# Two pairs of heads of batch 0: fp16 weight pairs turned by DMA in place of fp32 weights turned on TensorE, in a tuned attention + Mish MLP kernel

## The chip, the core and the metric

The kernel runs on one core of one Trainium2 chip. The metric is the device time of one execution in microseconds (us), the median over several runs. The core has five instruction streams: TensorE for matrix products (PE in the views, PEld for its weight loads), VectorE (DVE), ScalarE (ACT), GpSimd (POOL) and SyncE (SP), which here only issues DMA transfers. Each stream runs its instructions in the order in which the program holds them, and an instruction that waits holds up all that stand behind it on its stream.

## What is computed

Rotary attention over 4 batches, 8 heads, 576 positions of 64 numbers, and then an MLP with a Mish-like gate on the 2304 rows of 512 numbers that come out of it. All inputs and the output are fp32.

```python
q_rot, k_rot = (rotate(q), rotate(k))
scores = scale * np.matmul(q_rot, k_rot.transpose(0, 1, 3, 2))
scores = scores - np.max(scores, axis=-1, keepdims=True)
attn = np.exp(scores)
attn = attn / (np.sum(attn, axis=-1, keepdims=True) + 1e-09)
attn_out = np.matmul(attn, v)                # (4, 8, 576, 64)
x = attn_out.transpose(0, 2, 1, 3).reshape(2304, 512)
h = x @ w_in                                 # 512 x 2048
g = h * np.tanh(np.where(h > 20.0, h, np.log1p(np.exp(np.minimum(h, 20.0)))))
return g @ w_out                             # 2048 x 512
```

## The kernel before

**Attention.** The heads are taken in pairs, `P` = 0 to 15; pairs 0 to 3 are batch 0. One `step(P, t)` handles 128 queries of a pair; the fifth step, t = 4, handles the last 64 queries of two pairs at once. A step multiplies on PE (`scores`, line 502, into the two PSUM buffers `pair`), takes row maxima on DVE (L510), exponentials with their sums on ACT (L512, into `e`), and the inverse of the sums on DVE (L520, L522). The weights must then be turned, so that the keys lie on partitions, before `av` can multiply them by V. There are two ways:

- Batch 0 (`exact` in the code): `turned` turns the fp32 `e` by PE against a unit matrix (L546, and L561 for the last 64 keys), turns the inverse sums too (L563), and ACT or DVE copy the results out of PSUM into `et` and `ew` (L555/L556, L570/L572, L574/L576). `av` multiplies in fp32 (L630, L632, L633). DVE then multiplies by the inverse sums (L661), and `x` is written as a sum of two fp16 parts: the high part by L664 or L666, the rest on DVE (L669).
- The other batches: `weights_hi` writes weights times inverse sum as fp16 (L527 on POOL, L529 on ACT or L530 on DVE), `weights_lo` writes what fp16 lost as a second fp16 (L534, always DVE), a DMA issued by SP turns both at once (L617, from `ew` into `et`), and `av` makes three fp16 passes (L638, L642, L643), with V as an fp16 pair too (`load_v`, L463 to L467). The high part of `x` then comes straight from PSUM (L664 or L666), the rest by L669.

`av(P, k)` covers the first 256 queries (k = 0) or the last 320 (k = 1). `et` has two buffers and `ew` three, used in turn.

**MLP.** A chunk c is half a batch: 256 or 320 columns. `mlp_h` makes 16 groups of 12 matmuls (L877), the Mish on ACT (L882) and the fp16 pair `g` (L892/L893, L896); `mlp_p` makes 16 groups of 12 matmuls (L913) and writes the output. The weights arrive as fp32 and are taken apart into fp16 pairs by `decode` (L755 to L775), in the first third of the kernel. For batch 0 the two h chunks stand before the two p chunks in the plan's numbering, but PE's order mixes them with attention: h of the first 256 columns, then p of those, then h of the last 320 columns, which needs `x` of all four pairs with k = 1.

**Order.** Every operation has a number. A table, `ORDER`, lists the numbers in the order in which they are issued; a letter chooses one of the engines that an operation allows, `@` the PSUM banks, and `+m` puts m idle matmuls against the unit matrix (L1026) ahead of the operation on PE. All engines' streams follow from this one list.

Of the kernel before, what the change touches and what calls it, by code (L numbers as in the profile page):

```python
# [10 lines left out]
F32 = mybir.dt.float32  # L11
# [12 lines left out]
NP = H // 2  # L24
# [25 lines left out]
AVL = 3  # L50
PREP = [7, 5, 0, 13]
# [13 lines left out]
    205b 103@1 148 186@3 229@0 146 202 36 206 147 188 34 257b 150 233 149 251b 153@4+6 40 207 235 208 151 189 43 236@2
    104 237 37 230 458 105@3 41 238 285 192@2 35 107@1 245b 239 209 154 194 51 240@0 190 152 46 214@54 241 195 108 191
    109 106 242 286 244@0 157@1 203 196 215 159 158 287 216 217 288@2+6 197 155@3 357 289 218 246 169@1 52 170 297b
    290 356 270@54+3 459 250@2 247 156 47 291 172 256@1 273 292@0 337@3 271 274 49 252 272 293 220 253 231 53 248 258
    224@4 254 338 50 222@0 219 259 54 280@2 48 225 378 278@3 303b 309 322@54 460 223 221 275 377 55 529 281 279 226@1
    262@0 325 263 276 323 326 56 277 264 324 282@2+9 462 232 608 341@45 294 284 265 227 283 575 461 266 330@3 249  # L70
    296@2 342 373@0 18 344 228 331 394 379 343 463 315 339 406 298 637 345 349@1 267 464 613 327 374 260 465@3 530 328
    386 380@0 329 347 346 350 334@4 466 255 348 171 467 375 381 353@3 468 336 299 335 314@1 469@0 400 382 295 351@5
    387 383 355 470 354 316 412 384@2 352 332@0 385 317 308@3 358@45 376 333 120 389 310 617 300 454@2 361 302@1 638
    359 390 362 304 360 311 614 368@5 305 393@0 455 366@3 369 395 1 456 418@45 340 306 457 31 396 261 367 526@1 419
    411@2 307 421 420 635@0 210 363 243 422 413 211 527 414 667@4 312b 183 301b 426@3 550 313 636 546@2 268 471 364
    668 472 365 388 423 405@1 609 549 606@5 415 407 547 408 703@0 607 212 665b 399@2 701b 666 409 435@45 427b 410 704
    318 401 370@1 436 610 684@0 372 397 371b 402 416 437 213 438 428@3 825@1 615 429b 766 702 439 806@2 398b 826 424
    618 441 440 511@45 442 425 709 434 685 789@3 514 807 403 269 833b 430@1 804b 790 319b 449@0 515 431b 404 432b
    443@2 512 446@3 805 433 1094@1 450b 611 513 448 531@54 445 834 451 444 453 760 640 452b 447 829@2 532 499 474 533
    521@0 612 827 602@3 534 641 522 705 473 44 710 535 830 537 516 764 475 517 713 581c 476@0 603 541@5 518 487b 639  # L80
    477 539@3 391 320 478 542 479 523@2 714 540 480@0 57 880@4 711 481 604 536 525b 321 706 765 484 538 505 524b 519@3
    493b 828 543@0 881 482 520 605 831@5 483 545b 707b 504@2 544b 708 498@3 661@0 506 832 762 507 500 508 719 486@4
    501 839 509 502 488 914@2 878 662 503 489 492@3 587@54 915 879 528 616 494 490 835@0 590 918 491 495 591 1109 919
    588 842 837@2 485 723 589 840 392 510 593 836 620@45 548 1110 621 838 592 551 622 916b 595@3 917 597@0 623 552@2
    1137 553 624 554 555 496b 596 556@2 497 642@45 557 594 417 626 558 1138b 559 598 569 599@3 645 716 574@2 563 628@1
    718 643 601 0 1139 1140@0 576 600 577 1154 769 629b 568@3 578b 562@2 560 1155 579 646 564 570 663 1182 843 644 565
    625 571 630@1 1183 627 664 754b 669@54 647 566b 631 722 567 580@2 650@3 648 672 632@0 651 670 841 652 1185@1 673
    633b 572b 970 649 634 582 573 671 656@3 583 686@45 736 653@0 689 717 1199 654b 690 971 657b 748c 660 584 785@2 687
    659b 688 655b 585 720 712 691 692 561 675 721 972 658b 724 973 725@0 786 677@5 726 787 679@3 727 678 728 974 694@2
    680 729@0 772@45 695 1043 730 674 586 693 731 788 732 619 676 735@3 696@0 775 1200 742b 737 697 738 1184 681@2  # L90
    747@0 739b 1239 773 1044 776 682b 683b 774 749 698@3 1046 1240 791@54 699b 741@2 777 750 1045 1241 778 743 821@1
    700 751 740 794 753@0 744 795 752 792 745 779 755 781b 857 797 756 1242@3 793 768 746b 757 783 808@45 780b 733 758
    822 796 1256 823 798 811 799b 882 782 800b 1257 809 861 812 734 759 1281 810 886 802 824 883 844@54 888 801 784
    884 814 920@2 715 845 885 813 887 846 922@0 815 1282b 817b 1047 847 890 858 889 848 803 943@1 849 923 850 761 819
    864@54 859 944 891 862 921 964@3 1201 851 941 867 816 994 892 998 853 865 939@0 965 852c 868 855 958@1 818 942 820
    866 854 893@2 1048 901@45 870 990 1002 959b 894 869 995 960 924@3 904 999 856 871 895 905 896 902 988@2 1003 903
    1049b 925 897@1 873c 968@5 898 1000 899 872c 940 907 992@1 989 900 906 966b 1283 908 874 969 875 1020 1018@3 909b
    996b 876 967 926@45 911 993 910b 997 1156 1088@0 929 1019 1115 863 927 930 912 1041@2 1111 1321 1039b 1040 928
    961@1 1202b 1004 991 1089 931 1021 945@54 913 932 933 1203b 1042 934c 935b 1070@3 1204 946 962 963 947 948 1037@0
    1157 1334 877 949 936 1066@2 1038 937 951 1118 975@54 938 1335 860 1071 1022@1 1116 976 1067 950 1090 952 978 1159  # L100
    1284@0 1023 953b 1092b 977 1301 1068b 1093 1091 1085@3 979 955 954b 1069 1005@54 980 956 981 957 982 1302 1216 983
    1008 1006 984 1009 985 1317 1007 986 1338 1217 1119 1024@45 1011 987 1086b 1318 1010 1012 1117 1320@2 1027 1014
    1025 1028 1013 1339 1362 1026 1160 1030 1112 1029 1016 1001 1050@54 1015 1120 1319 1031 767 1033 1032b 1063@1 1053
    1158 1051 1054 771 1121 1052 1034 1113 1017 1072@45 1056 1322 1055 1035 1161 1363 1114 1075 1073 1076 1057 1036
# [178 lines left out]
def attention_mish_mlp(ctx: ExitStack, tc: tile.TileContext, qk, v, vflat, rope, ident_in, w_in, w_out, outT):  # L283
# [807 lines left out]
```

## Time and profile before

| | |
|---|---|
| time before, median of 3 runs | 614.68 us (614.17 to 615.95) |
| the profiled execution | 615.46 us, of which the span from first to last instruction is 613.7 us |
| PE busy in the span | 592.6 us (97%) |
| DVE / ACT / POOL busy | 447.2 / 390.9 / 239.9 us |
| mean granted TensorE clock | 0.997 of full speed |

A busy share counts an instruction from its start to its end. PE's instructions overlap in the array, so its share says little of how closely they follow each other; for that the starts of neighbouring rows are compared.

### The profile page before, as it was taken

Reading aid. Unit: us, or ns where it says so; the run is one execution under the profiler, and the core shown is the slowest. Engines: PE = TensorE matmul, PEld = TensorE weight load, DVE = VectorE, ACT = ScalarE, POOL = GpSimd, SP = SyncE. Lnnn points to the kernel's source line nnn. Section 1 sums busy time; section 2 is a strip of 40 time slices with the busy share of each in tenths; the row PEclk is TensorE's granted clock in tenths of the full one; section 3 lists DMA queues with packets and bytes.
Section 4 is the critical chain, followed back from the end, with each engine's and each line's share of the span. In section 5 each row is a group of like instructions: output and inputs, shape, how many; then the busy total and the mean of one; then the engine's idle time right before and its main releaser. Section 6 shows DMA issues by size and latency. Waiting matters only on the chain. (4 is left out here: it accounts for less than half of the span.)

```text
span 613.7 us, 12945 instructions
## 1 busy us (share of the span) xinstructions
PE 592.6 (97%) x5112; PEld 442.8 (72%) x5112; DVE 447.2 (73%) x964; ACT 390.9 (64%) x771; POOL 239.9 (39%) x218
## 2 busy tenths in 40 slices
PE   5889999999999999999999999999999999999997
PEld 4655776776666666788877767887877778887775
DVE  4999998998899989678788976678878754320320
ACT  3799998978879665587768454765689534311400
POOL 2989567556645555341762006208221010000000
PEclk9989999999999999999999999999999999999999
DMA  9977234242879689917792866355745773100000
GB/s 341 409 296 263 76 112 160 69 151 70 209 178 237 133 184 204 194 21 155 181 168 40 193 122 135 90 117 101 129 89 87 139 136 69 31 10 1 27 12 33
DMA packets 143436, 82.49 MB, mean 134 GB/s; under 512 B 128144, under 2 KB 133904, under 8 KB 141712
## 3 DMA queue, kind: packets, MB, share of 16 engines
q1 hardware_dynamic: 138768, 76.95, 52.1%
q10 hardware_dynamic: 4608, 4.72, 2.3%
q8 instruction: 40, 0.66, 0.4%
q14 instruction: 20, 0.16, 0.1%
HBM read 45.09 MB, written 4.72 MB: 81 GB/s over the span
## 5 line engine op out<-in xcount | busy, mean ns | idle before, releaser
L913 PEld LDWEIGHTS <-w 128*128 128x128 f16 x1536 | 147.2, 98 | 46.2 <-issue 9.8
L877 PEld LDWEIGHTS <-w 128*128 128x128 f16 x1536 | 148.0, 98 | 42.8 <-issue 7.2
L913 PE MATMUL bank<-g,w 128*128 128x320 f16 (+1 forms) x1344 | 176.0, 288 | 0.0
L877 PE MATMUL bank<-xt,w 128*128 128x320 f16 (+1 forms) x1284 | 166.8, 286 | 0.1
L512 ACT ACTIVATE e<-pair,mx 128x576 f32<-128x576 f32 x144 | 105.8, 738 | 66.8 <-DVE mx L510 61.4
L510 DVE TENSOR_REDUCE mx<-pair 128x1 f32<-128x576 f32 x144 | 104.9, 747 | 27.9 <-PE pair L502 27.6
L386 POOL TENSOR_TENSOR raw<-raw,cs 128x576 f32<-128x576 f32 (+2 forms) x62 | 94.3, 1538 | 74.3 <-DMA raw<-in_qk 70.3
L534 DVE SCALAR_TENSOR_TENSOR ew<-e,rs,ew 128x576 f16<-128x576 f32 x108 | 104.8, 988 | 4.5 <-ACT ew L529 3.4
L502 PE MATMUL pair<-qk 64*128 64x288 f32 (+1 forms) x704 | 84.2, 366 | 1.1 <-ACT e L512 0.5
L527 POOL TENSOR_SCALAR ew<-e,rs 128x576 f16<-128x576 f32 x33 | 27.0, 819 | 146.2 <-DVE rs L522 79.8
L882 ACT ACTIVATE mh<-bank,cells 128x320 f32<-128x320 f32 (+1 forms) x107 | 50.5, 498 | 37.7 <-PE bank L877 25.1
L502 PEld LDWEIGHTS pair<-qk 64*128 64x128 f32 (+1 forms) x704 | 54.3, 181 | 21.5 <-issue 10.1
L896 DVE SCALAR_TENSOR_TENSOR g<-mh,cells,g 128x640 f16<-128x640 f32 (+1 forms) x56 | 49.2, 894 | 14.6 <-ACT g L892 14.4
L893 DVE TENSOR_SCALAR g<-mh,cells 128x640 f16<-128x640 f32 (+1 forms) x32 | 16.9, 533 | 51.3 <-ACT mh L882 35.5
L529 ACT ACTIVATE ew<-e,rs 128x576 f16<-128x576 f32 x44 | 33.7, 769 | 15.5 <-issue 9.8
L643 PE MATMUL bank<-et,v 128*64 128x256 f16 (+1 forms) x288 | 39.8, 288 | 0.0
L642 PE MATMUL bank<-et,v 128*64 128x256 f16 (+1 forms) x288 | 39.8, 288 | 0.0
L642 PEld LDWEIGHTS <-v 128*64 128x64 f16 x288 | 29.6, 110 | 8.4 <-issue 5.7
L882 ACT ACTIVATE mh<-pair,cells 128x256 f32<-128x256 f32 (+1 forms) x21 | 10.4, 495 | 36.8 <-PE pair L877 31.8
L877 PE MATMUL pair<-xt,w 128*128 128x256 f16 (+1 forms) x252 | 33.9, 284 | 0.0
L882 ACT ACT_TABLE_LOAD x24 | 30.8, 1283 | 1.4 <-DVE xt L896 0.4
L390 POOL TENSOR_TENSOR raw<-raw 128x288 f32<-128x288 f32 x32 | 31.1, 985 | 0.3
(142 smaller groups left out, 770.2 us busy)
## 6 DMA issues: line engine op xcount, KB each, us to landing
raw<-in_qk SPq DMA_DIRECT2D x30, 576.0 KB, 4.5
w<-in_w_out SPq DMA_DIRECT2D x5, 1024.0 KB, 5.2
g<-in_w_in SPq DMA_DIRECT2D x4, 1024.0 KB, 6.5
w<-in_w_in SPq DMA_DIRECT2D x4, 1024.0 KB, 8.8
stg<-in_v SPq DMA_DIRECT2D x8, 320.0 KB, 4.0
out_dram<-ot ACTq DMA_DIRECT2D x16, 160.0 KB, 2.2
stg<-in_vflat SPq DMA_DIRECT2D x6, 384.0 KB, 3.8
qk<-in_w_out SPq DMA_DIRECT2D x4, 512.0 KB, 4.7
```

Source lines behind the costliest of these rows:

```text
L386: e.tensor_tensor(out=t()[:, :, s], in0=t()[:, :, s], in1=cs()[:, :, s], op=ALU.mult)
L502: nc.tensor.matmul(pts[h]()[to, c, :HS], x[own, q], y[own, s], **kw)
L510: op((DVE, dve_ns(S), lambda: nc.vector.tensor_reduce(m(), pt()[:, :, :HS], axis=AX.XY, op=ALU.max, negate=True)), w=[m], r=[pt])
L512: op((ACT, act_ns(S, psum=True, ptr=2) + 35, lambda: nc.scalar.activation(e().rearrange("p (c s) -> p c s", c=2), pt()[:, :, :HS], AF.Exp, ...
L529: (ACT, act_ns(S, ptr=1) + 25, lambda: nc.scalar.activation(w()[:, c], e(), AF.Copy, scale=r()[:, h:h + 1])),
L534: op((DVE, dve_ns(S) + 130, lambda: nc.vector.scalar_tensor_tensor(out=w()[:, c], in0=e(), scalar=r()[:, h:h + 1], in1=w()[:, hc], op0=ALU ...
L642: nc.tensor.matmul(po()[0:64, :n], V()[:, vi, c, 0:64], et[:, c, :], start=False, stop=last)
L643: nc.tensor.matmul(po()[64:128, :n], V()[:, vi, c, 64:128], et[:, 5 + c, :], start=False, stop=last)
L877: nc.tensor.matmul(hp(), w1()[:, wi, cc, f:f + 128], x()[:, xi, cc, q0:q0 + n], start=cc == 0 and a == 0, stop=cc == NCC - 1 and a == 2)
L882: op((ACT, act_ns(n, psum=True, ptr=1) + 60, lambda j=j, hp=hp: nc.scalar.activation(hn()[:, j, :n], hp(), AF.Mish, scale=uh())), w=[(hn, ...
L896: op((DVE, dve_ns(2 * n) + 61, lambda: nc.vector.scalar_tensor_tensor(out=gv()[:, 1, f, :n], in0=hn()[:, :, :n], scalar=f32(gs), in1=gv()[ ...
L913: nc.tensor.matmul(pp()[:, :n], w2e[e]()[:, wi, f], gv()[:, gi, f % 4, :n], start=f == 0 and a == 0, stop=f == NF - 1 and a == 2)
```

## The change

A new constant `NX = 2` says for how many pairs of batch 0 the last 320 queries keep the exact way. Pairs 2 and 3 lose it for k = 1, that is for five steps: t = 2 and 3 of each, and their shared t = 4. V of these two pairs is read from memory a second time and taken apart into an fp16 pair (`cast_v`, at two new places of the program). And `ORDER` is another table throughout: other places, engines, banks and fills.

```diff
+NX = 2
@@ load_v
-        t, flat = v_stage(P // NP)
+        cast_v(P)
+
+    def cast_v(P):
+        t, flat = v_stage(max(1, P // NP))
...
-        st["V", P] = o
+        st["H", P] = o
@@
+    def exact(P, k):
+        return P < NP and (k == 0 or P < NX)
+
@@ places
-            et_tile(p, k, *((F32, 9) if P < NP else (F16, 18)))
-            if P < NP:
+            et_tile(p, k, *((F32, 9) if exact(p, k) else (F16, 18)))
+            if exact(p, k):
@@ step
-        exact = P < NP
+        own = exact(P, int(t > 1))
         to = places(P, t)
-        ew = None if exact else sbuf((128, 4 * S), F16, "ew", EW)
+        ew = None if own else sbuf((128, 4 * S), F16, "ew", EW)
...
-        if exact:
+        if own:
             turned(es, [(st["ET", p, k], at, t, st["R", p, k], q) for p, k, at, q in to], r)
             return
@@ av
-        V = st["V", P]
+        V = st["V" if exact(P, k) else "H", P]
@@
         at(2 * P - 4, load_v, P)
     at(VA, v_amax, 0)
+    for P in range(NX, NP):
+        at(12 + P, cast_v, P)
@@ ORDER, two of its rows
-    59 2 58 3 5 11 6 4 20 140b 111 12 134c 94 122b 110 128b 19 112 113@0+16 32 7b 114 115 116 117@1+7 118 13 119 9
+    588 509 492@3 830@2 502 545b 544b 494 486@1 503 660@0 495 589 484 590 528 912 637 496b 591 488 497 831 592 717
```

In what follows the changed kernel's lines stand 3 to 8 further down than before: scores are L505, the maxima L513, `weights_lo` L537, the turning DMA L623, fp16 `av` L644/L648/L649, the second MLP product L919, the fills L1034.

On PE, in the stretch of the second MLP product of batch 0's first 256 columns, before the change (`e_...` are the exponentials of single heads, `bank` and `pair` PSUM buffers):

```order
L913 MATMUL bank_73<-stg,w_68 128x256
L546 MATMUL bank_74<-ident,e_1444 128x128 x4
L502 MATMUL pair_78<-qk 128x288
L502 MATMUL pair_77<-qk 128x288
...
L546 MATMUL bank_76<-ident,e_1560 128x128 x4
L561 MATMUL bank_73<-ident,e_1415 64x128
L561 MATMUL bank_73<-ident,e_1444 64x128
L563 MATMUL bank_73<-ident,rs 64x128 x2
L913 LDWEIGHTS w_68
```

The same stretch with the change:

```order
L919 MATMUL bank_73<-stg,w_68 128x256
L1034 LDWEIGHTS ident
L1034 MATMUL pair_78<-ident 128x256
...
L505 MATMUL pair_78<-qk 128x288
L505 MATMUL pair_77<-qk 128x288
...
L919 LDWEIGHTS w_68
L919 MATMUL bank_73<-stg,w_68 128x256
```

The turning groups are gone between the MLP groups; ahead of four operations here stand fills, of 5, 5, 5 and 4 matmuls, one of which is shown. The whole program holds 147 fill matmuls where it held 124.

On DVE, the end of the exact work of these two pairs before the change:

```order
L510 TENSOR_REDUCE mx<-pair_78 128x1
L556 COPY et<-bank_73 128x4x64
L572 COPY et<-bank_76 128x64
L759 TENSOR_SCALAR raw<-raw 128x512
L510 TENSOR_REDUCE mx<-pair_77 128x1
L572 COPY et<-bank_76 128x64
L556 COPY et<-bank_73 128x4x64
L722 TENSOR_REDUCE cells<-qk 128x1
```

And with the change, about there:

```order
L537 SCALAR_TENSOR_TENSOR ew<-e_1566,rs,ew 128x576
L537 SCALAR_TENSOR_TENSOR ew<-e_1521,rs,ew 128x576
L513 TENSOR_REDUCE mx<-pair_78 128x1
L513 TENSOR_REDUCE mx<-pair_77 128x1
L767 SCALAR_TENSOR_TENSOR bank_74<-bank_74,qk 128x512
L537 SCALAR_TENSOR_TENSOR ew<-e_1650,rs,ew 128x576
L537 SCALAR_TENSOR_TENSOR ew<-e_1645,rs,ew 128x576
L770 SCALAR_TENSOR_TENSOR qk<-qk,bank_74 128x512
```

Copies out of PSUM have given way to two L537 for each step, ten in all. Counted between the first L877 matmul on 256 columns and the first on 320 in the list, DVE has these differences: nine L534 more (the tenth comes after), four more pieces of `decode` (L761, L764, L775), six L572, five L893, two L661, three L836 and one each of L556, L759 and L922 fewer, and four more of the shortest (L336, L520, L522); L893's five went to ACT as L892.

On SP, the first turning DMAs with the change, among the loads of weights and of q and k:

```order
L715 DMA raw<-in_w_out 128x512
L715 DMA qk<-in_w_out 128x512
L623 DMA_TRANSPOSE et<-ew 128x18x128 x2
L623 DMA_TRANSPOSE et<-ew 128x18x64
L380 DMA raw<-in_qk 128x1152
L715 DMA qk<-in_w_out 128x512
L623 DMA_TRANSPOSE et<-ew 128x18x64
```

Before the change no turning DMA stands among the loads of `w_out`; six have come to stand in and behind them.

## Rows read from the trace of the kernel before

**Rows 1.** The page: the span.
```profile
span 613.7 us, 12945 instructions
```

**Rows 2.** Windows: busy time of each engine in one stretch.
```profile
core 0: us, PE busy (x) PEld busy (x) DVE busy (x) ACT busy (x) POOL busy (x), PEclk, DMA share, GB/s
71.70:158.90 87.20, 85.92 (x730) 63.39 (x729) 79.33 (x212) 75.31 (x154) 53.47 (x48) 1.00 0.34 112
```

**Rows 3.** Timeline of PE: first h matmuls on 256 and on 320 columns (start, us, instruction).
```profile
71.70 2.79 PE L877 MATMUL bank<-xt,w 128*128 128x256 f16 x24
...
158.94 1.26 PE L877 MATMUL bank<-xt,w 128*128 128x320 f16 x8
```

**Rows 4.** Timeline of PE: turning in fp32, and what follows it.
```profile
142.45 0.66 PE L546 MATMUL bank<-ident,e 128*128 128x128 f32 x4
142.94 1.47 PE L913 MATMUL bank<-stg,w 128*128 128x256 f16 x12
144.35 0.44 PE L561 MATMUL bank<-ident,e 128*64 128x128 f32 x4
...
144.94 1.48 PE L913 MATMUL bank<-stg,w 128*128 128x256 f16 x12
```

**Rows 5.** Timeline of PE: an fp32 `av` on 320 queries, first row and next work.
```profile
148.11 0.81 PE L630 MATMUL bank<-et,v 128*128 128x320 f32 x2
...
151.15 1.48 PE L913 MATMUL bank<-xt,w 128*128 128x256 f16 x12
```

**Rows 6.** Timeline of PE: an fp16 `av` on 320 queries, first row and next work.
```profile
213.63 0.58 PE L638 MATMUL bank<-et,v 128*128 128x320 f16 x3 [0.60 <-DMA et<-ew]
...
215.89 1.00 PE L502 MATMUL pair<-qk 64*128 64x288 f32 x6
```

**Rows 7.** Timeline of PE: a fill and what follows it.
```profile
43.47 0.83 PE L1026 MATMUL bank<-ident 128*128 128x256 f16 x6
44.14 0.27 PE L346 MATMUL bank<-ident,cells 128*1 128x128 f32 x1
```

**Rows 8.** Groups of DVE, 71.7 to 158.9 (busy us, mean ns | idle before).
```profile
L510 DVE TENSOR_REDUCE mx<-pair 128x1 f32<-128x576 f32 x24 | 17.7, 749 | 2.2 <-PE pair L502 1.9 <-ACT qk L398 0.2
L764 DVE SCALAR_TENSOR_TENSOR w<-w,bank 128x512 int32<-128x512 int32 x9 | 6.1, 682 | 0.1
L534 DVE SCALAR_TENSOR_TENSOR ew<-e,rs,ew 128x576 f16<-128x576 f32 x4 | 3.2, 810 | 0.0
L572 DVE COPY et<-bank 128x128 f32<-128x128 f32 (+1 forms) x11 | 2.8, 255 | 0.2 <-PE bank L563 0.2
L661 DVE TENSOR_TENSOR ew<-bank,ew 128x320 f32<-128x320 f32 x4 | 1.9, 482 | 0.0
L893 DVE TENSOR_SCALAR xt<-mh,cells 128x512 f16<-128x512 f32 x3 | 1.4, 478 | 0.0
```

**Rows 9.** `weights_lo` in the whole span, and one beside a POOL instruction.
```profile
L534 DVE SCALAR_TENSOR_TENSOR ew<-e,rs,ew 128x576 f16<-128x576 f32 x108 | 104.8, 988 | 4.5 <-ACT ew L529 3.4 <-POOL ew L527 0.8
...
181.62 1.88 POOL L467 TENSOR_TENSOR v<-raw,v 128x640 f16<-128x640 f32 x1 [2.45 <-DVE v L466]
...
182.17 1.95 DVE L534 SCALAR_TENSOR_TENSOR ew<-e,rs,ew 128x576 f16<-128x576 f32 x1
```

**Rows 10.** Waits of DVE, 71.7 to 158.9 (us in total, times, longest).
```profile
DVE cells L355 <- PE bank L352: 2.3, 3, 1.0
DVE mx L510 <- PE pair L502: 1.9, 4, 1.1
```

**Rows 11.** Windows of 10 us: DVE later, where it is fullest (columns as in 2).
```profile
180.00:190.00 10.00, 10.00 (x84) 6.59 (x83) 9.93 (x17) 8.11 (x15) 1.88 (x1) 1.00 0.72 215
190.00:200.00 10.00, 10.00 (x74) 6.90 (x73) 9.57 (x16) 9.87 (x16) 8.03 (x5) 1.00 1.10 187
```

**Rows 12.** Turning DMAs, issue to landing; waits of PE for them, and of SP.
```profile
DMA to landing us min/median/max: 3.8/4.7/9.8
...
PE bank L638 <- DMA et<-ew: 2.1, 2, 1.5
...
SPq L709 <- PE pair L502: 13.6, 2, 11.1
```

More of the change, by code (lines that the diff above doesn't have):

```diff
@@ L65 @@
[L65 to L79, printed above, removed]
@@ L600, in step @@
     def step(P, t):
-        exact = P < NP
+        own = exact(P, int(t > 1))
         to = places(P, t)
-        ew = None if exact else sbuf((128, 4 * S), F16, "ew", EW)
+        ew = None if own else sbuf((128, 4 * S), F16, "ew", EW)
         sm = sbuf((128, 2), F32, "sm", 3)
         es = [max_exp(pt, h, sm) for h, pt in enumerate(scores(P, t))]
-        r = inverse(sm, 2, 1.0 if exact else 2.0 ** -15)
-        if exact:
+        r = inverse(sm, 2, 1.0 if own else 2.0 ** -15)
+        if own:
             turned(es, [(st["ET", p, k], at, t, st["R", p, k], q) for p, k, at, q in to], r)
@@ L626, in av @@
         need = ([0, 1], [2, 3, 4])[k]
-        exact = P < NP
+        own = exact(P, k)
         def exact_fn():
@@ L643, in fn @@
                     nc.tensor.matmul(po()[64:128, :n], V()[:, vi, c, 64:128], et[:, 5 + c, :], start=False, stop=last)
-        if exact:
+        if own:
             need = [(t, a) for t in ([0, 1], [2, 3, 4])[k] for a in range(3)]
@@ L652, in av @@
         x = st["x", b]
-        sv = sc["v", b][1] if exact else None
+        sv = sc["v", b][1] if own else None
         def scale():
-            return f32(sv) if exact else 2.0 ** -15
-        if exact:
+            return f32(sv) if own else 2.0 ** -15
+        if own:
             R = st["R", P, k]
@@ L662, in av @@
                w=keys, r=[po])
-        px, po_ = (R, keys) if exact else (po, [po])
-        op([(ACT, act_ns(n, psum=not exact, ptr=int(exact)), lambda: nc.scalar.activation(
+        px, po_ = (R, keys) if own else (po, [po])
+        op([(ACT, act_ns(n, psum=not own, ptr=int(own)), lambda: nc.scalar.activation(
             x()[:, 0, p, q0:q0 + n], px()[:, :n], AF.Copy, scale=scale())),
             (DVE, dve_ns(n) + 61, lambda: nc.vector.tensor_scalar(
-                x()[:, 0, p, q0:q0 + n], px()[:, :n], scale(), None, op0=ALU.mult), *[1] * exact)],
-           w=[(x, (p, k, 0))], r=po_ + [sv] * exact)
-        op((DVE, dve_ns(n) + 61 * exact, lambda: nc.vector.scalar_tensor_tensor(
+                x()[:, 0, p, q0:q0 + n], px()[:, :n], scale(), None, op0=ALU.mult), *[1] * own)],
+           w=[(x, (p, k, 0))], r=po_ + [sv] * own)
+        op((DVE, dve_ns(n) + 61 * own, lambda: nc.vector.scalar_tensor_tensor(
             out=x()[:, 1, p, q0:q0 + n], in0=px()[:, :n], scalar=scale(), in1=x()[:, 0, p, q0:q0 + n],
-            op0=ALU.mult, op1=ALU.subtract), *[1] * exact), w=[(x, (p, k, 1))], r=po_ + [(x, (p, k, 0))] + [sv] * exact)
+            op0=ALU.mult, op1=ALU.subtract), *[1] * own), w=[(x, (p, k, 1))], r=po_ + [(x, (p, k, 0))] + [sv] * own)
     def v_amax(b):
```

192 lines of the change are left out of this document (103 added, 89 removed).

## The prediction, made blind

> **What bounds the kernel now.** I read the page first: the span is 613.7 us [rows 1], and PE is busy for 97% of it. A busy share hides how closely matmuls follow each other, so I went on to the windows and the timeline of PE. The reader is to see one stretch there, from the first h matmul on 256 columns at 71.70 us to the first on 320 columns at 158.94 [rows 3]. All five steps that the change touches lie in it, and nothing of the change's fp32 work lies outside. In this stretch PE is busy 85.92 of 87.2 us, DVE 79.33, ACT 75.31 [rows 2]. So PE ends last, but DVE has only 7.9 us to spare and ACT 11.9. Behind 158.94 the same PE work stands before and after the change, so a gain has to come as an earlier start of the h matmuls on 320 columns. DVE's waits in the stretch say who held whom: its largest are for PE, 2.3 and 1.9 us [rows 10].
>
> **What PE loses.** A turning group of four transposes runs from 142.45 to the next work at 142.94, 0.49 us; the group of L561 and L563 from 144.35 to 144.94, 0.59 us [rows 4]. Five steps hold ten of the first and five of the second: 4.9 + 2.95 us. An fp32 `av` on 320 queries takes 148.11 to 151.15, 3.04 us [rows 5]; an fp16 one 213.63 to 215.89, 2.26 us [rows 6]. Two of them give 1.56 us. Together 9.4 us of PE. Against it stand the fills. Six take 43.47 to 44.14, 0.112 each [rows 7], and the 19 in this stretch 2.1 us. They are no loss by themselves, since a fill stands where PE has nothing else; but they are on PE's stream and run whether it is so or not. PE's floor for the stretch is then 87.2 - 9.4 + 2.1 = 79.9 us.
>
> **What DVE gains.** The counts are those of the order (the section on the change). Nine `weights_lo` at 0.81 us [rows 8] are +7.3; four more pieces of the taking apart of weights at 0.68 [rows 8] +2.7. Away go six copies at 0.255, five L893 at 0.478 and two L661 at 0.482 [rows 8]: -4.9. The other six removed and the four short ones added I take at -1.5 together, by the same rows as the nearest (L572 and L893 for length). The sum is +3.6 us, so DVE has 82.9 us of work ahead of the same point. ACT trades copies for `weights_hi` and five g pieces; its spare 11.9 us covers the few us that this costs, and it sets nothing unless DVE is wrong by as much.
>
> The upper bound of a `weights_lo` is not 0.81. Over the whole span its mean is 988 ns, and beside a POOL instruction that ran from 181.62 to 183.50, one that began at 182.17 took 1.95 us [rows 9]: it ended 0.62 us after POOL's. At 988 the nine cost 1.6 us more and DVE's work is 84.5. The four in this stretch now ran at 810 though POOL was busy 53.47 of 87.2 us [rows 2, 8], so I take the lower value and keep the upper for the range. The Trainium skill (SBUF — State Buffer, section "SBUF: two separate sides") says that DVE with two SBUF inputs and a POOL instruction that reads SBUF exclude each other for a whole instruction. The pair of rows above agrees with it; by the rule alone, every `weights_lo` that meets POOL would wait, and the sum would be the upper one.
>
> **What the stretch then takes.** DVE's 82.9 us lie above PE's 79.9. So PE stops setting this stretch and DVE does, and of PE's 7.3 us only what DVE can follow is won. How full can DVE be? Where it is fullest later, it is busy 9.57 to 9.93 of 10 us [rows 11]. Its waits for PE, 4.2 us in the two largest rows [rows 10], should mostly go, since PE now has time to spare. Full, DVE takes 82.9; at 9.57 of 10 it takes 86.6. I take 98%, 84.5 us, nearer to the full end because the waits that held it were PE's. The gain is 87.2 - 84.5 = 2.7 us. The work moved out of its old place elsewhere costs nothing by this count: ahead of 71.7 us the order holds as much DVE work as before, to 0.1 us by the same durations, and behind 158.94 PE's list is the same. Both parts were searched anew, though, and small waits will differ: I allow 1.5 us either way.
>
> **The turning DMAs** add six transfers, landing after 4.7 us in the median, 9.8 at most [rows 12]. The stretch has 24 maxima [rows 8], two for each step, so a step comes every 7.3 us, and `av` stands three steps behind its last scores: 22 us. `weights_hi`, `weights_lo` twice and the landing take about 8 of them. The rest is cover, and if it is used up, each further us delays the h matmuls by one. The DMA engines are busy for a share of 0.34 here [rows 2]. The Trainium skill (VectorE: DVE Perf Modes, "The three transpose paths") speaks against the change: it gives 390 ns for a 128 by 128 turn on TensorE and 1309 by DMA, and advises TensorE when the result may go to PSUM. As an estimate from its figures, 18 tiles of a step would take 23.6 us one after another, and there would be no cover; the landing row says 4.7.
>
> **The sum.** The profiled execution took 615.46 us, 1.8 outside its span. 615.46 - 2.7 = 612.8 for that one; it lies 0.8 above the median of the runs. Against the median, 614.68 - 2.7 = **612.0 us**, or 0.4% less. A difference of 0.3%, 1.8 us, is about what a measurement of this kernel tells from none; that is below 612.8 or above 616.5.
>
> **Rivals.**
> - *PE's saving comes in full.* DVE work can slip behind the start of the h matmuls, which need only the last L669. For it: a few of DVE's instructions just ahead of that start serve later steps. Against it: rows 2 leave DVE too little. 614.7 - 7.3 = 607.4 us.
> - *Nothing is won.* The `weights_lo` meet POOL more often and DVE is full to 9.57 of 10: 84.5 / 0.957 = 88.3 us, +1.1; or to 98%, 86.2, -1.0. The time is 613.7 to 615.8 us.
> - *DVE keeps its pauses: slower.* If the 7.9 us without work stay, because the chain of maxima, exponentials, inverse and `weights_lo` holds DVE at each step as PE did, the stretch takes 82.9 + 7.9 = 90.8 us, +3.6, and the time is 618.3. It decides from 4.3 us of pauses. For it: PE has little other work there, as the fills show; against it: the windows of [rows 11].
> - *The turned weights come late: slower.* SP stood up to 11.1 us at a load of `w_out` into a `qk` buffer, for scores on PE [rows 12], and the first turning DMAs now stand right behind such a load. Cover of some 14 us is lost if two such stops meet; PE already waits 2.1 us in two `av` later on [rows 12]. Above 14 us, 2 to 5 us more: 616.7 to 620.
>
> **Chances.** Forecast 0.42, its own range 610.5 to 613.2; full saving 0.17; nothing won 0.19; pauses stay 0.12; turned weights late 0.10. Faster by over 0.3%: full saving and five sixths of the forecast, 0.52. Within 0.3%: the rest of the forecast and nearly all of "nothing won", 0.25. Slower: both slower rivals and a little, 0.23. The range goes from 607.0, where the full saving lies, to 617.5; it leaves out half of the slower cases and the lower part of the full saving, about 0.19.
>
> **What would show it.** In the new profile the first h matmul on 320 columns should stand at 154.5 to 157.5 us instead of 158.94. Between the first h matmul and it, DVE should be busy for 82 to 85 us, 97% or more of the stretch; PE should show gaps or slow starts ahead of scores of about 4 us with the fills, and 9.4 us less turning and `av` work. `weights_lo` in the stretch should average near 0.81 us; near 1.0 would move the time by 1.6. A start near 151.6 would mean the full saving, with DVE instructions put off behind it. I am wrong in the mechanism if DVE has pauses of over 4 us there, if PE waits for `et`, or if the difference arises ahead of 71.7 or behind 158.94.

## The result, and the profile after

The changed kernel takes 618.9 us (median of 9 runs, 617.0 to 620.4); the kernel before, run beside it, 615.3 (9 runs). The ratio is 1.0053, 95% interval 1.0034 to 1.0073: slower by 0.5%, 3.3 us. The prediction said 612.0 and faster, so its sign is wrong, and the time lies above its range. The profiled execution of the changed kernel took 618.88 us, its span 616.8.

The timeline of PE after the change, at the first h matmul on 256 columns and the first on 320; it answers to [rows 3].

```profile
72.14 1.04 PE L883 MATMUL bank<-xt,w 128*128 128x256 f16 x8
...
162.51 0.72 PE L883 MATMUL bank<-xt,w 128*128 128x320 f16 x4
```

The second mark stands at 162.51 us instead of 158.94. The stretch between the marks takes 90.4 us instead of 87.2; ahead of it the new kernel is 0.4 us later, behind it 0.5 us shorter (616.8 - 162.5 = 454.3 against 454.8). So the loss arises where the prediction looked for the gain. The windows of the changed kernel, with the columns of [rows 2]: the stretch, the next one up to the second h on 256 columns, and a few tens of us.

```profile
72.10:162.50 90.40, 84.74 (x692) 62.11 (x690) 85.72 (x210) 78.34 (x152) 57.96 (x52) 0.96 0.53 143
162.50:254.40 91.90, 90.48 (x732) 60.03 (x731) 85.56 (x163) 70.39 (x136) 54.06 (x46) 1.00 0.89 200
...
130.00:140.00 10.00, 6.88 (x60) 4.51 (x58) 8.54 (x19) 7.49 (x16) 6.41 (x6) 1.00 0.85 197
140.00:150.00 10.00, 9.50 (x51) 6.47 (x52) 9.04 (x19) 6.09 (x12) 5.44 (x6) 0.66 0.60 137
```

The reader is to see three things. DVE is busy 85.7 us of the stretch: 6.4 more than before, not 3.6, and 4.7 us are left in which it has nothing to do. PE has gaps from 130 to 140 us. And from 140 to 150 the granted clock is 0.66: for a part of it PE ran at 1.2 GHz instead of 2.4. The waits of DVE in the stretch say what its 4.7 us were spent on; they answer to [rows 10].

```profile
DVE cells L728 <- DMA qk<-in_w_out: 1.4, 1, 1.4
DVE mx L513 <- PE pair L505: 1.1, 2, 0.7
DVE mx L513 <- ACT mh L888: 0.8, 1, 0.8
...
DVE cells L355 <- PE bank L352: 0.2, 1, 0.2
```

The timeline of PE shows the place where it stood and the clock fell.

```profile
136.02 1.48 PE L919 MATMUL bank<-stg,w 128*128 128x256 f16 x12
139.08 0.27 PE L346 MATMUL bank<-ident,cells 128*1 128x128 f32 x1 [1.57 <-DVE cells L343]
140.50 0.58 PE L352 MATMUL bank<-ident,cells 1*128 1x1 f32 x2 [1.16 <-DVE cells L336]
141.01 2.29 PE L505 MATMUL pair<-qk 64*128 64x288 f32 x8
143.24 4.71 PE L919 MATMUL bank<-xt,w 128*128 128x256 f16 x24
147.88 1.24 PE L505 MATMUL pair<-qk 64*128 64x288 f32 x8
```

PE stands for 2.7 us at the exponent of the last quarter of `w_out` (L346, L352). The scores behind take 2.29 us, where the next ones take 1.24, and 24 p matmuls 4.71. What PE waited for is followed back through DVE, SP and POOL (timelines of each):

```profile
125.87 3.16 DVE L537 SCALAR_TENSOR_TENSOR ew<-e,rs,ew 128x576 f16<-128x576 f32 x2
128.96 0.68 DVE L770 SCALAR_TENSOR_TENSOR qk<-qk,bank 128x512 int32<-128x512 int32 x1
...
138.14 0.69 DVE L728 TENSOR_REDUCE cells<-qk 128x1 f32<-128x512 f32 x1 [1.43 <-DMA qk<-in_w_out]
```
```profile
123.97 1.97 POOL L530 TENSOR_SCALAR ew<-e,rs 128x576 f16<-128x576 f32 x2 [2.08 <-ACT stg L898]
125.91 1.40 POOL L470 TENSOR_TENSOR v<-raw,v 128x640 f16<-128x640 f32 x1
127.39 1.04 POOL L763 TENSOR_SCALAR w<-w 128x512 int32<-128x512 uint32 x1
130.47 1.16 POOL L781 TENSOR_TENSOR w<-qk,w 128x512 f16<-128x512 f32 x1 [2.04 <-ACT w L777]
```
```profile
120.31 0.33 SPq L715 DMA_DIRECT2D qk<-in_w_out  x1
120.75 9.57 SPq L623 DMA_TRANSPOSE et<-ew  x3
130.41 1.34 SPq L380 DMA_DIRECT2D raw<-in_qk  x1
131.88 0.35 SPq L715 DMA_DIRECT2D qk<-in_w_out  x1
```

Two `weights_lo` (L537) stood beside POOL's L470 and L763 and took 3.16 us together instead of 1.62. The step behind them on DVE (L770) is one of the decoding of another `w_out` piece, whose end on POOL (L781, done at 131.63) frees the `qk` buffer for the last piece. That load was issued at 131.88, landed at 138.1, and DVE's maximum of it began then. SP's three turning DMAs hold its stream from 120.75 to 130.3, but they ended before POOL did, so it was not they that held this load.

The groups of DVE in the stretch: `weights_lo`, which answers to [rows 8].

```profile
L537 DVE SCALAR_TENSOR_TENSOR ew<-e,rs,ew 128x576 f16<-128x576 f32 x13 | 13.4, 1054 | 0.0
```

Thirteen of 1.054 us on average keep DVE busy for 13.4 us (neighbours overlap a little), against 3.2 us for four of 0.81 before. The nine more cost 10.2 us and not 7.3.

### The profile page after: what moved, and what is told of

Its sections match the earlier page's. It is cut to its first block, busy times and chain, and to the rows that moved or that the text cites. A ratio compares the mean times of both kernels' runs of the same rounds, so it can differ in the third digit from the quotient of the medians.

```text
span 616.8 us, 12860 instructions
## 1 busy us (share of the span) xinstructions
PE 591.1 (96%) x5073; PEld 440.7 (71%) x5073; DVE 458.0 (74%) x964; ACT 392.1 (64%) x767; POOL 249.5 (40%) x222
## 4 chain that ended last, share of the span: by engine, by line
PE 70%; DVE 17%; DMA 5%; ACT 5%; issue 2%; SPq 1%; POOL 0%; DVEq 0%; ACTq 0%
PE bank L883 25%; PE bank L919 24%; PE pair L505 9%; PE bank L648 5%; DVE ew L537 4%; DVE mx L513 4%; PE pair L883 3%; DMA g<-in_w_in 2%; DMA et<-ew 2%; DVE cells L728 1%; PE bank L644 1%; ACT e L515 1%; DVE bank L767 1%; DMA qk<-in_w_out 1%; PE bank L638 1%
## 5 line engine op out<-in xcount | busy, mean ns | idle before, releaser
L919 PEld LDWEIGHTS <-w 128*128 128x128 f16 x1536 | 147.7, 98 | 48.4 <-issue 10.0
L883 PE MATMUL bank<-xt,w 128*128 128x320 f16 (+1 forms) x1380 | 178.3, 286 | 0.0
L919 PE MATMUL bank<-g,w 128*128 128x320 f16 (+1 forms) x1344 | 175.7, 288 | 0.0
L513 DVE TENSOR_REDUCE mx<-pair 128x1 f32<-128x576 f32 x144 | 104.4, 747 | 23.6 <-PE pair L505 22.5
L537 DVE SCALAR_TENSOR_TENSOR ew<-e,rs,ew 128x576 f16<-128x576 f32 x118 | 117.7, 1010 | 4.5 <-ACT ew L532 4.2
L386 POOL TENSOR_TENSOR raw<-raw,cs 128x576 f32<-128x576 f32 (+2 forms) x61 | 89.7, 1481 | 57.1 <-DMA raw<-in_qk 51.1
L888 ACT ACTIVATE mh<-bank,cells 128x320 f32<-128x320 f32 (+1 forms) x115 | 54.6, 499 | 64.9 <-PE bank L883 57.7
L505 PE MATMUL pair<-qk 64*128 64x288 f32 (+1 forms) x704 | 86.1, 366 | 3.4 <-ACT e L515 2.7
L530 POOL TENSOR_SCALAR ew<-e,rs 128x576 f16<-128x576 f32 x35 | 32.8, 940 | 135.4 <-DVE rs L525 92.5
L505 PEld LDWEIGHTS pair<-qk 64*128 64x128 f32 (+1 forms) x704 | 55.2, 182 | 24.9 <-issue 10.3
L899 DVE TENSOR_SCALAR g<-mh,cells 128x640 f16<-128x640 f32 (+1 forms) x32 | 20.0, 624 | 35.5 <-issue 19.0
L648 PE MATMUL bank<-et,v 128*64 128x320 f16 (+1 forms) x312 | 43.4, 289 | 0.0
L649 PE MATMUL bank<-et,v 128*64 128x320 f16 (+1 forms) x312 | 43.4, 289 | 0.0
L648 PEld LDWEIGHTS <-v 128*64 128x64 f16 x312 | 32.1, 110 | 9.4 <-issue 6.2
L390 POOL TENSOR_TENSOR raw<-raw 128x288 f32<-128x288 f32 x32 | 35.3, 1116 | 0.5
L649 PEld LDWEIGHTS <-v 128*64 128x64 f16 x312 | 32.1, 110 | 0.0
L523 DVE TENSOR_SCALAR sm<-sm 128x1 f32<-128x1 f32 x144 | 18.6, 144 | 17.4 <-ACT e L515 17.1
```

The costliest lines, as they stand in the source:

```text
L386: e.tensor_tensor(out=t()[:, :, s], in0=t()[:, :, s], in1=cs()[:, :, s], op=ALU.mult)
L390: e.tensor_tensor(out=to, in0=t()[:, 0, s], in1=t()[:, 1, s], op=ALU.add)
L505: nc.tensor.matmul(pts[h]()[to, c, :HS], x[own, q], y[own, s], **kw)
L513: op((DVE, dve_ns(S), lambda: nc.vector.tensor_reduce(m(), pt()[:, :, :HS], axis=AX.XY, op=ALU.max, negate=True)), w=[m], r=[pt])
L537: op((DVE, dve_ns(S) + 130, lambda: nc.vector.scalar_tensor_tensor(out=w()[:, c], in0=e(), scalar=r()[:, h:h + 1], in1=w()[:, hc], op0=ALU ...
L648: nc.tensor.matmul(po()[0:64, :n], V()[:, vi, c, 0:64], et[:, c, :], start=False, stop=last)
```

## The experiments

Fifteen kernels were run, each timed in five rounds beside the kernel before; the ratios below are to that one, with 95% intervals. The stretch is always from the first h matmul on 256 columns to the first on 320.

### Is it the order of the changed kernel?

Theory A was the row of events above: a late piece, a stop and half the clock. Theory B was DVE's work. In the table `ORDER` a row is an operation's number, a letter for its engine, `@` its banks and `+` its fills. 720 and 724 are the transpose and the broadcast of the last exponent.

```diff
- ... 567b 584 720@3
- 721 709 1176 689 560 722 1177 723 690 706 782 724@0 692b 767@54 ...
+ ... 567b 584 720@3+13
+ 721 709 1176 689 560 722 1177 723 690 706 782 724@0+9 692b 767@54 ...
```

> The changed kernel with 13 more fills ahead of the transpose of the last w_out exponent and 9 ahead of its broadcast: PE works on through the 2.7 us for which it stood there (137.5 to 140.5 us); nothing else is moved. Theory A, a late piece and the clock: the last quarter of w_out comes late on PE's stream, PE stands, the granted clock falls, and scores and p behind it run at half speed (2.29 us for 1.24, 4.71 for 2.78). With the clock held, 3.0 us come back: 615.9 us, h on 320 columns from 159.5. Theory B, DVE: DVE's 85.9 us of work set the 90.4 us of the stretch and PE only waits for it; in the slow piece DVE stands 0.7 us, so no more than that comes back: 618.2 to 618.9 us, h on 320 columns from 161.8 or later.

Measured: 618.8 us, 1.0045 (1.0026 to 1.0064). The clock held, and the pieces behind the stop ran at full speed (timeline of PE):

```profile
141.44 1.24 PE L505 MATMUL pair<-qk 64*128 64x288 f32 x8
142.61 2.79 PE L919 MATMUL bank<-xt,w 128*128 128x256 f16 x24
```

The stretch became 87.4 us, 3.0 less, as theory A had it. The time did not follow: h on 320 columns started 2.2 us earlier, but the next stretch took 93.5 us instead of 91.9 (the two windows of this run).

```profile
72.89:160.31 87.42, 84.44 (x714) 62.84 (x712) 83.77 (x210) 78.08 (x152) 57.92 (x52) 1.00 0.57 144
160.31:253.83 93.52, 91.73 (x733) 60.20 (x732) 83.69 (x164) 70.45 (x136) 54.39 (x46) 1.00 0.94 199
```

So the prediction's rule that an earlier start of these h matmuls is a gain does not hold by itself. Right behind the mark ACT stood for a V load, with two exponentials queued behind it (timeline of ACT in this run):

```profile
163.11 0.83 ACT L466 ACTIVATE raw<-raw,cells 128x640 f32<-128x640 f32 x1 [2.41 <-DMA raw<-in_v]
```

The changed kernel's own runs say the same of the clock: one of the nine had a mean granted clock of 1.000, and it took 618.4 us. So the loss can stand without the half clock.

The second kernel releases the late piece earlier: 577 is the L770 row above and 579 the L781 row.

```diff
- ... 655 670 656 1131 568@2 1133@1+5
- 657 569b 577 640 658 1147 671 578 570 672 563 571 704 580@0 683@54+4 579 715 ... 712
+ ... 655 670 577 656 1131 568@2 1133@1+5
+ 657 569b 658 1147 671 578 570 672 571 580@0 683@54+4 579 640 563 715 ... 712 704
```

> The changed kernel with the last piece of w_out released and loaded earlier: on DVE the last step of the piece that holds its buffer (L770) goes ahead of two weights_lo, on POOL the rest of that piece (L781) goes ahead of a V cast (L470) and a low part (L763), on SP the load goes ahead of a q load. The two weights_lo then also meet no POOL work (now 2.04 and 1.19 us instead of 0.81). Theory A: the stop of 2.7 us and the half clock behind it (3.0 us) both go: about 613.2 us. Theory B: what DVE gains counts, 1.6 us of contention, 1.4 us of its own wait for the piece and 0.7 us in the slow piece: 615.2 to 615.9 us.

Measured: 619.2 us, 1.0063 (1.0045 to 1.0082). The two `weights_lo` took 0.81 each, and the clock did not fall. But the 14 `weights_lo` between 72.1 and 162.5 us still averaged 1.046 us: the meetings with POOL went to others. The stretch became 88.4 us and the next one 92.5; in the time nothing was won, against both theories.

The third kernel shortens DVE's new work instead.

```diff
+    def copy_lo(w, part, hpart, c, hc, e, r, h):
+        op((DVE, dve_ns(S) + 130, lambda: nc.vector.tensor_copy(w()[:, c], w()[:, hc]), 1),
+           w=[(w, part)], r=[e, (r, h), (w, hpart)])
-            weights_lo(ew, 2 + h, h, ...
+            (copy_lo if P < NP else weights_lo)(ew, 2 + h, h, ...
```

> The changed kernel with the ten weights_lo of the moved steps replaced by a plain fp16 copy of weights_hi on the same engine at the same place (the low part of these weights is left out). This takes perhaps 0.6 us off each and DVE's lock against POOL with it. Theory B, DVE sets the stretch: 6 to 7 us less on DVE come back until PE is the bound again, 612 to 613 us, h on 320 columns from 156 or earlier. Theory A, the late piece sets it: the piece comes at most 2 us earlier, because its buffer is released behind two of these weights_lo, and the clock may still fall: 615.5 to 617 us.

Measured: 618.0 us, 1.0045 (1.0027 to 1.0064). The copies took 0.41 us each, DVE's busy time in the stretch fell from 85.7 to 80.2 us, and the stretch stayed at 90.2: its pauses grew from 4.7 to 10 us, at the same late piece and behind the same half clock. (The profiled execution was the slowest of the twelve, 621.0 us, so in the median run the stretch may have been shorter.) Theory B in its plain form, and theory A alone, had both failed.

The fourth takes out the 19 fills.

```diff
- 646@54+5   668@54+5   1133@1+5   683@54+4
+ 646@54     668@54     1133@1     683@54
```

> The changed kernel without the 19 fills that the change adds in the stretch. If they stand where PE waits in any case and the clock does not need them (both theories in their plain form): 618.9 us within 0.6. If they cost what they take on PE's stream, 2.1 us: 616.8 us. If they hold the clock through PE's waits at 118 to 130 us, it falls there without them and scores and p run at half speed: 621 us or more.

Measured: 621.8 us, 1.0093 (1.0070 to 1.0115). For the whole kernel the fills are not a cost of 2.1 us; without them it is slower by 0.4%, with intervals that just touch. The windows of this run show the granted clock in three places, where the changed kernel has 1.00, 0.66 and 1.00, and then the stretch and the next one:

```profile
130.00:140.00 10.00, 7.96 (x58) 5.18 (x58) 8.66 (x22) 7.60 (x16) 6.66 (x6) 0.83 0.81 184
140.00:150.00 10.00, 9.68 (x72) 7.23 (x74) 9.92 (x26) 8.47 (x18) 7.36 (x7) 1.00 0.90 184
240.00:250.00 10.00, 10.00 (x66) 6.00 (x65) 7.69 (x15) 4.75 (x11) 5.27 (x5) 0.73 0.89 163
71.93:159.47 87.54, 82.51 (x674) 59.73 (x671) 83.94 (x210) 78.37 (x152) 57.92 (x52) 0.98 0.55 145
159.47:257.01 97.54, 95.01 (x733) 61.65 (x732) 86.82 (x164) 70.55 (x136) 55.21 (x46) 0.97 0.94 190
```

Without the fills the stretch itself is 2.9 us shorter than in the changed kernel (87.5 against 90.4), and the next one 5.6 us longer. The loss is behind the stretch, part of it at the lower clock.

Next came the gate behind the stretch. 876 and 877 are the V cast (L466, L468), 839 and 841 the exponentials; the edit with the fills of the first kernel, the edit alone, and the edit with the fills and the copies of the third.

```diff
- 795 837@45 ... 936@0 838 876 811 754 1275 796 0 877 913@1 881 840 965 839 797 841 966 ...
+ 795 837@45 ... 936@0 838 811 754 1275 796 0 913@1 881 840 965 839 797 841 876 877 966 ...
```

> Holding the clock brought h on 320 columns forward by 2.2 us, and the time did not move: behind 160 us ACT stood 2.4 us at the cast of a V load that landed at 163.1 as before, and two exponentials were queued behind it. This kernel holds the clock in the same way and puts that cast and the next one behind the two exponentials on ACT. Theory C, gates in a row: this cast was the second gate, so about 2 us come back: 616.7 us. Theory D, a bound that lies further on: av waits for its turned weights up to 238.5 us in every version so far (238.9, 238.5, 238.7, 239.3), and eats what comes earlier: 618.8 us, with a longer wait of av at 238 us.

> The changed kernel with only the V cast and the one behind it put behind the two exponentials on ACT. In the changed kernel DVE stood 0.9 us for the exponential there and scores on PE 0.6 us: 618.0 to 618.5 us by theory C, 618.9 by theory D.

> Clock held, the V cast behind the exponentials, and the ten weights_lo replaced by short copies (the low part of these weights is left out): all three suspects gone at once. If the stretch was held by DVE together with them (copies alone gave nothing: 618.0 us): 611 to 613 us, h on 320 columns from 155 or earlier. If turned weights at 238 us set the time (theory D): 617 to 619 us, and PE waits there for more than 4 us.

Measured: the cast moved alone, 618.3 us, 1.0029 (1.0003 to 1.0055). With the clock held, 617.8 us, 1.0020 (0.9996 to 1.0045); the next stretch still took 93.4 us, so the cast was not the whole of that gate. The sign of the other theory, a longer wait of `av` for its turned weights near 238 us, did not come either: it was 1.10 us in the changed kernel, 1.09 with clock and cast repaired and 0.82 with the copies as well. With the copies as well, 616.1 us, 0.9995 (0.9973 to 1.0017): the time of the kernel before, between the two forecasts, and an interval that does not touch that of the changed kernel, though it does touch that of the two repairs. With the two repairs and most of DVE's new work cut, the loss is gone; but nothing of PE's 7.3 us came out even then. All three order repairs together, with the work left whole:

```diff
+ ... 655 670 577 656 1131 568@2 1133@1+5
+ 657 569b 658 1147 671 578 570 672 571 580@0 683@54+4 579 640 563 715 ... 712 704
+ ... 720@3+13 721 709 ... 782 724@0+9 692b ...
+ ... 797 841 876 877 966 ...
```

> The changed kernel with all three repairs of its order that keep the result: clock held by 22 fills, the V cast behind the exponentials on ACT, the last w_out piece released earlier and two weights_lo away from POOL. If each gate gave what it cost: 615.5 to 616.5 us. If the contention only moves to other weights_lo, as when the piece alone came earlier: 617.5 us, like the first two repairs.

Measured: 617.9 us, 1.0048 (1.0031 to 1.0066). The repairs do not add up. In the profiled executions the stretch took 87.4 us with the clock held, 88.4 with the early piece, 87.5 without the fills, 87.4 with clock and cast and 88.1 with all three, all within 1.2 us of the 87.2 before; but the next stretch took 93.5, 92.5, 97.5, 93.4 and 94.8, against 91.5 before and 91.9 in the changed kernel. What was won ahead of the h matmuls on 320 columns was lost behind them, and no run here shows what holds that next stretch.

### What is a microsecond of each engine worth in the stretch?

These runs leave the orders as they are and change the work of one engine in the five moved steps. First the kernel before with PE's saving alone.

```diff
-    def turned(es, to, r):
+    def turned(es, to, r, n4=4):
-                for c in range(4):
+                for c in range(n4):
-            turned(es, [...], r)
+            turned(es, [...], r, 1 if P >= 2 and t >= 2 else 4)
             # and in the fp32 av:
+            n4 = 1 if P >= 2 and k == 1 else 4
-            for c in range(4):
+            for c in range(n4):
```

> The kernel before, with PE's saving alone: in the five steps that the change moves, each turning group does one of its four transposes, and the two fp32 av take one of four chunks (three quarters of these steps' weights are left out). That takes 30 x 0.122 + 2 x 2.07 = 7.8 us from PE in the stretch, and nothing is added to DVE, ACT, POOL or the queues, and nothing moved. If PE sets the stretch and DVE follows to 98 per cent, as the prediction had it: 80.9 us of stretch at most 6.3 less, 609 us. If what PE loses turns into waits for exponentials at each step (DVE's and ACT's chain sets the pace there already): 613 us or more.

Measured: 615.4 us, 0.9993 (0.9964 to 1.0022). Then DVE's share alone, and both at once.

```diff
+    more = fixed((128, 1), F32, "more")
-        op((DVE, 100, lambda: nc.vector.reciprocal(r()[:, 0:n], sm()[:, 0:n])),
+        def last():
+            nc.vector.reciprocal(r()[:, 0:n], sm()[:, 0:n])
+            for e in es:
+                nc.vector.tensor_reduce(more(), e(), axis=AX.X, op=ALU.max)
+        op((DVE, 100, last),
```

> The kernel before with DVE's share of the change alone: ten more maxima over 128x576 (about 0.7 us each, their results unused) in the same five steps, right behind the reciprocal, as the weights_lo come in the changed kernel: some 7 us, about what DVE's work grew by in the stretch (79.3 to 86.0 us). Theory F, DVE's ordered work sets the pace of the stretch and its pauses are chains that stay: 4 to 7 us slower, 619.5 to 622.5 us. Theory G, DVE has 7.5 us without work there and PE covers it: 615.5 to 617 us.

> Both shares at once in the order of before: 7.8 us less on PE as in the run with less PE work (three quarters of these steps' weights left out) and the ten maxima on DVE. No turned DMA, no new fp16 work, no new order. If engine work alone explains the changed kernel (theory F): as slow as it or slower, 618 to 621 us. If its loss is the new order's late piece, clock and V cast: 615 to 616.5 us.

Measured: 624.0 us, 1.0137 (1.0117 to 1.0157), with DVE's share; 622.1 us, 1.0108 (1.0086 to 1.0130), with both. The ten maxima took 0.742 us each, 7.4 together, and cost 8.4 us. Both times lie above theory F's ranges. The windows of the stretch in these three runs, in the order less PE, more DVE, both:

```profile
71.10:157.00 85.90, 81.44 (x677) 59.49 (x677) 79.61 (x212) 75.42 (x154) 53.18 (x48) 1.00 0.34 113
```
```profile
70.60:167.10 96.50, 89.61 (x731) 64.22 (x731) 88.89 (x223) 76.37 (x155) 53.70 (x50) 0.98 0.31 101
```
```profile
70.00:165.00 95.00, 87.53 (x677) 61.84 (x677) 89.09 (x222) 75.75 (x154) 53.39 (x49) 0.95 0.32 103
```

Length less DVE's busy time is DVE's pause: 7.9 us before [rows 2], then 6.3, 7.6 and 5.9. Taking 7.8 us from PE shortened the pauses by 1.6 us, and work put on DVE hardly went into them. The granted clock of the three stretches is 1.00, 0.98 and 0.95, so part of what the added work cost may be the clock's. The waits of DVE in the run with less PE work say which stayed; they answer to [rows 10].

```profile
DVE cells L355 <- PE bank L352: 1.7, 3, 1.0
DVE mx L510 <- PE pair L502: 1.5, 4, 0.7
```

Before, these were 2.3 and 1.9. The first is a wait inside a chain (a maximum goes from DVE to PE and back twice), and less work on PE took only 0.6 us from it; the second is a wait for scores, and it lost 0.4. In this run PE itself stood 1.96 us at the same L346 at 136 us, for DVE.

Is DVE then the one bound, also downward? The next kernel takes work off it: 15 small copies of turned weights go to ACT.

```diff
- 431b 432b 450b 452b 525b 524b 545b 544b 633b 657b 659b 658b 682b 683b 699b
+ 431  432  450  452  525  524  545  544  633  657  659  658  682  683  699
```

> The kernel before with 15 of the 16 small copies of turned weights in the stretch (0.26 us each on DVE) on ACT instead, where such a copy takes about as long; nothing else is moved. DVE loses 3.8 us, ACT takes 3.8 of its spare 11.9. Adding 7 us to DVE cost 8 to 9 us. Theory F, DVE's ordered work sets the pace in either direction: 611 to 612.5 us. Theory G, DVE and PE are level before the change (the run with less PE work gained 1.4 us in the stretch at most): less DVE work alone gains nothing either, 614.5 to 616 us. A copy that now waits its turn behind exponentials on ACT would make it slower, 616 us or more.

Measured: 618.1 us, 1.0032 (1.0015 to 1.0049): slower. The stretch took 89.6 us. DVE's busy time did not even fall (the window of the stretch, and below it two groups of DVE in the stretch):

```profile
70.20:159.80 89.60, 86.64 (x731) 63.43 (x731) 80.37 (x196) 77.75 (x169) 53.10 (x48) 1.00 0.34 109
```
```profile
L534 DVE SCALAR_TENSOR_TENSOR ew<-e,rs,ew 128x576 f16<-128x576 f32 x4 | 4.0, 1001 | 0.0
L896 DVE SCALAR_TENSOR_TENSOR xt<-mh,cells,xt 128x512 f16<-128x512 f32 x4 | 3.9, 963 | 0.0
```

The `weights_lo` were 810 ns in the kernel before [rows 8] and are 1001 here, and the `xt` form of L896 went from 806 to 963: with one L772 and one L759 that became longer beside POOL, some 3.5 us of the copies' 3.8 came back. The copies on ACT have a price too, as the third forecast said (waits in the stretch of this run):

```profile
DVE bank L761 <- ACT bank L755: 2.7, 3, 2.1
...
PE bank L913 <- ACT ew L574: 1.3, 1, 1.3
...
PE bank L630 <- ACT et L570: 0.9, 1, 0.9
```

Before, DVE waited at that place for 0.2 us, and no matmul of PE waited for a copy on ACT. So this run does not show what less DVE work is worth, since DVE had no less. The last three runs put work on either engine, in either kernel.

```diff
 # changed kernel, more DVE: inverse() as above, for the steps of P < NP without own
 # changed kernel, more PE: the fp16 av of P < NP
-            passes = [... for vi, ei in ((0, 0), (1, 0), (0, 1))]
+            passes = [... for vi, ei in ((0, 0), (1, 0), (0, 1))] * (2 if P < NP else 1)
 # kernel before, more PE: turned() with twice = 2 in the five steps
-                for c in range(4):
+                for c in [*range(4)] * twice:
-            for h, a in ((0, 512), (1, 0)):
+            for h, a in ((0, 512), (1, 0)) * twice:
```

> The changed kernel with ten more maxima over 128x576 on DVE (0.7 us each, unused) in the moved steps, as they were put into the kernel before, where they cost 8 to 9 us. If DVE's ordered work holds the stretch of the changed kernel: 7 us or more, 626 us. If a late piece, the clock or the turned weights hold it and DVE has room: at most 3 us, 622 us.

> The changed kernel with the two fp16 av of the moved heads run through their three passes twice (the products of these heads are doubled): 2 x 2.2 = 4.4 us more on PE, in two pieces in the stretch, and no other engine has more to do. If PE's time in the stretch is free, as its waits of 5.7 us and the fills say: 618.9 to 620 us. If PE holds it as well: 623 us.

> The kernel before with the transposes of the five steps done twice (into the same banks) and the two products behind them as well: 10 x 0.49 + 5 x 0.30 = 6.4 us more on PE in the places from which the changed kernel and the run with less PE work took some. If PE sets the stretch of the kernel before, as the prediction read from its 98.5 per cent: 6 us, 621.5 us. If PE and DVE are bound into one chain, in which less of either wins nothing and more of either costs: 619 to 622 us. If PE has room there because DVE sets it: 615.5 to 617 us.

Measured: 623.4 us, 1.0109 (1.0079 to 1.0140); 621.1 us, 1.0089 (1.0061 to 1.0118); 619.4 us, 1.0055 (1.0035 to 1.0075). In the changed kernel 7.4 us more on DVE cost 3.4 us beyond its own loss (0.0056 of 615.8), 4.4 more on PE 2.2 (0.0036, with intervals that overlap, so less surely). Both lie between the two forecasts. In the kernel before, 6.4 us more on PE cost 3.4. The window of the stretch in that last run:

```profile
71.10:163.80 92.70, 91.54 (x790) 69.08 (x789) 80.34 (x211) 76.24 (x154) 53.31 (x48) 1.00 0.33 105
```

PE is busy 98.7% of it (98.5% before, [rows 2]), and DVE's pauses are 12.4 us. So PE counts upward and DVE counts upward. Downward, less PE work alone was worth nothing in the kernel before, and less DVE work alone nothing clear in the changed one (the copies); in the kernel before no run brought DVE's work down.

## Why the prediction was wrong

**What PE loses.** The counts held: no fp32 turning is left of the five steps. What it is worth did not. With the 7.8 us taken off PE and nothing else touched, the stretch shortened by 1.3 us and the time by 0.4, with an interval on both sides of none. This part of the prediction already said that only what DVE can follow is won. The run shows that the rest of the stretch, with DVE's work as it was, could follow by 1.3 us.

**The fills** were put down as 2.1 us on PE's stream. Taking them out made the stretch shorter (87.5 us) and the kernel slower by 0.4%, and the granted clock fell to 0.83 and 0.73 in two windows where it had been 1.00, while it rose from 0.66 to 1.00 in a third. So as a cost the term may hold inside the stretch, but the whole kernel is slower without the fills; why the next stretch then loses more is not shown in full.

**What DVE gains** is the first term of the sum that was mis-sized: 6.4 us measured, 3.6 predicted. The difference, 2.8 us, is the length of `weights_lo`: 10.2 us for nine, not 7.3, above even the upper value of the prediction. The four in the kernel before had been at 0.81 although POOL was busy for 53.5 of 87.2 us, and the prediction took that for the rule. In that trace they began while POOL was idle or about to end, and it was POOL's instruction that became longer: an L775 that began 0.2 us behind a `weights_lo` took 1.62 us, the one ahead of it 1.17. The Trainium skill (SBUF — State Buffer, section "SBUF: two separate sides") says that DVE with two SBUF inputs and a POOL instruction that reads SBUF lock each other out for whole instructions, and that the one that starts first goes on. The trace agrees: 3.16 us for two of them beside two POOL instructions. The prediction weighed that rule against four rows and kept the rows; here it should have priced the new `weights_lo` by it.

**How full DVE can be** is the second term, and the step that failed: "I take 98%, 84.5 us, nearer to the full end because the waits that held it were PE's". (82.9 us at 98% is 84.6; the 0.1 changes nothing.) Measured is 94.8% (85.7 of 90.4). With less PE work DVE's pauses in the kernel before went from 7.9 to 6.3 us only, so time to spare on PE does not by itself end the waits that name PE. In the changed kernel, with its new order, they did shrink (L355 from 2.3 to 0.2 us, the maxima's from 1.9 to 1.1), but a DMA wait of 1.4 and one for ACT of 0.8 took their place. The step also made the stretch follow from DVE's work alone: with 5.5 us of that work taken off again (the copies), the profiled stretch was as long as ever and the pauses 10 us. Work and pauses together are the 5.9 us between the predicted 84.5 us and the measured 90.4: 2.8 and 3.1.

**The turning DMAs** cost what was said: between 110 and 165 us landing took 5.3 us in the median, 8.0 at most, and PE waited for no `et` of the moved steps in the changed kernel (for 0.84 us at one `av` with the early piece). The rival on late weights fell. The Trainium skill's 1309 ns for a 128 by 128 turn by DMA (VectorE: DVE Perf Modes, section "The three transpose paths") would have made 23.6 us of a step's 18 tiles, as an estimate; the landing rows disagree.

**The rivals.** "DVE keeps its pauses: slower" gave 90.8 us of stretch and 618.3 us and said that it decides from 4.3 us of pauses. Measured: 90.4 us, 618.9 us, 4.7 us. It had 0.12. That its time came so near is luck: its DVE work was 2.8 us too small and its pauses 3.2 too large, and the two cancel. The signs that the prediction named for being wrong (pauses over 4 us; `weights_lo` near 1.0) are both there.

**What stays open.** Which part of the 3.3 us belongs to the late piece, the half clock and the V cast of the new order is not settled: their repairs moved the ratio by +0.0010 to -0.0033, and each interval overlaps that of the changed kernel. Nor is it settled how much DVE's new work has of it. With most of that work cut and nothing else the loss stayed (1.0045), with two repairs and nothing else it was 1.0020, and with both it was gone (0.9995); the last two intervals overlap. Work of about that size added to the kernel before, in its old order, slows it by 6.6 to 8.4 us, with PE's saving or without, so DVE's work is enough for a loss there; that it makes this one is argued and not shown. What holds the stretch behind the h matmuls on 320 columns, which took back what the repairs won, stays open. No version was faster than the kernel before.

## What to carry to other kernels

Two engines that hand work to each other in a fixed order can both be near their limit: here, in the kernel before, 7.8 us taken off one of them were worth nothing that could be measured, and a microsecond added to either cost about half of it or more. An earlier start in the middle of a kernel is no gain until the end of the kernel shows it. A change that trades engine time must be priced by what it adds, and what it saves only as far as a run with the saving alone shows it. Before a wait is put down to the engine that it names, see whether that engine was busy or whether the wait is a round trip; the round trips here gave back 0.6 of 2.3 us when PE alone got 7.8 us less to do. And two-input DVE work beside a busy POOL is priced at its contended length, unless the order is known to keep them apart.

## What was not expected of the hardware

- A turning DMA holds SP's stream far longer than a load: three took 9.57 us (SP timeline above), the load of `w_out` ahead of them 0.33. The q and k load that is next in SP's order went out behind them, at 130.41 us.
- PE's granted clock fell behind a stop of 2.7 us with one small transpose in it, and the 8 scores and 24 p matmuls behind it took 7.0 us instead of 4.0; 22 fills in the stop prevented it. That was worth 3.0 us in the stretch and nothing at the end.
- Moving 3.8 us of copies from DVE to ACT left DVE's busy time where it was (79.3 to 80.4 us), because other DVE instructions became longer beside POOL, some 3.5 us of it in four groups.
